# Attention outputs on quarters of TensorE: two PSUM banks for two units, and their weights fetched in one transfer

## The chip, the cores and the metric

The kernel runs on one core of a Trainium2 chip. The metric is the device time of one execution in microseconds (us); the kernel before takes 574.62 us, the median of three runs (573.59 to 574.97). TensorE (PE) multiplies matrices, VectorE (DVE), ScalarE (ACT) and GpSimd (POOL) work on elements, and SyncE (SP) issues nearly all DMA transfers from one queue, in order. TensorE writes only into PSUM, which has eight banks of 2 KB per partition.

## The reference, cut to what matters

```python
# q, k, v: (4, 8, 768, 64); 8 memory keys/values per head; chunks of 32 queries
for c in range(nc):
    k_ctx = k[:, :, max(0, c*32 - 16):min(S, c*32 + 32 + 8)]      # v_ctx likewise
    k_full = np.concatenate([mem_k, k_ctx], axis=2)               # 64 keys or fewer; v_full likewise
    scores = scale * np.matmul(q_c, k_full.transpose(0, 1, 3, 2))
    a = np.exp(scores - np.max(scores, axis=-1, keepdims=True))
    a = a / (np.sum(a, axis=-1, keepdims=True) + 1e-09)
    out[:, :, c_start:c_end] = np.matmul(a, v_full)               # the product that is changed
x = out.transpose(0, 2, 1, 3).reshape(B * S, H * D)
h = x @ w_in                                                      # (3072, 512) @ (512, 2048)
g = np.maximum(h, 0.0) + alpha * np.minimum(h, 0.0)
y = g @ w_out
```

Each chunk of 32 queries sees 64 keys: 16 to its left, its own 32, 8 to its right and the 8 memory keys.

## The kernel before, in words

The 3072 tokens are worked in eight half-sequences of 384 (`BT`). A *unit* is one half-sequence of two heads, so there are 32 units of twelve chunks each: four tiles of 96 queries (`TQ`), three chunks to a tile. Units 0 to 7 (`windows`) are worked in the first 30 us on their own path. Units 8 to 31 are the *later units*, and the change concerns these alone. They go in twelve pairs (`attend`), and of each pair:

- `head_products` (L425) multiplies 32 queries with their 64 keys, 24 matmuls per unit, each on 64 rows and 32 columns of TensorE; `scores` and `weights` make the softmax on DVE, ACT and POOL.
- `turn` transposes the weights of the two units on DVE into the tile `et` and writes them to DRAM (`far_e`); `fetch_turned` reads them back as `pt` with the keys on partitions. Before, a tile of 96 queries has its 104 keys and some more on 128 partitions, so every chunk's 64 keys go to another place among them (`PIECES`, four transfers) and the rest of `pt` is zero (`zero`, one memset on POOL at the sixth step of the first block, `CLEAR`).
- `value_products` (L528) multiplies the values `v_t` (loaded by `load_v` from `vw`) with `pt`: per unit eight matmuls (four tiles, two heads), each 128 keys by 64 dimensions with 96 columns of queries. Head 0 writes partitions 0 to 63, head 1 partitions 64 to 127. Each unit has one PSUM bank of its own (`bank`).
- `copy_raw` (L602) copies the unit's 384 columns from PSUM to SBUF on ACT, where POOL and ACT make further forms of them.

Most of TensorE's time goes to the two large products in fp32r as sums of three matmuls (high and low parts): L840 and L870 for the first blocks, L1311, L1418, L1274 and L1372 for the others, which use sums and differences of weight blocks.

The order on every engine is written by a planner (`Plan`): a step has an engine, a cost, what it reads and writes and how far it is from the end (`behind`), and the planner plays the steps through, on each engine taking the ready step with the largest `behind`. `SHIFT` adds a number to single steps, by name and count, and so moves them within the order. A planned cost is only what the planner reckons with.

Of the kernel before, what the change touches and what calls it, by code (L numbers as in the profile page):

```python
# [62 lines left out]
PIECES = [(0, 0, KW, 0), (1, 0, KW, CH), (2, 0, WIN, 2 * CH + NM), (2, WIN, KW, CH)]  # L63
# [54 lines left out]
CLEAR = 5  # L118

# [12 lines left out]
NV = NT * 2 * D  # L132

# [6 lines left out]
SHIFT = {("load_head", 1): 1.6, ("load_head", 7): 1.5, ("load", 0): 4.1, ("load", 4): -11.2, ("load", 15): 3,  # L140
         ("top", 0): 3, ("inverse", 0): -4.5, ("scale", 0): -1.5, ("scale", 1): -18, ("low", 0): -106.4,
         ("score_products", 1): 15, ("scale", 3): -12, ("keep", 2): -3, ("low", 1): 5.9, ("top", 2): 3,
         ("exps", 2): 3, ("total", 2): 1.5, ("inverse", 2): -0.8, ("scale", 5): 0.8, ("turn", 3): 6, ("keep", 6): 3,
         ("values", 3): 0.8, ("high", 3): 1.5, ("less", 4): -61.5, ("turn", 4): 6, ("values", 4): -12,
         ("keep", 11): -1.5, ("low", 5): -0.8, ("keep", 13): 6, ("high", 6): -11.2, ("total", 7): 0.8,
         ("keep", 15): -3, ("low", 7): 12.8, ("load", 22): 1.5, ("load", 28): 12, ("ends", 0): 9.8, ("up", 2): -1.5,
         ("low", 10): -12, ("gather", 2): 2.3, ("up", 15): 6, ("rebias", 4): -1.5, ("gather", 5): -21.7,
         ("ends", 4): 6, ("gather", 7): -3, ("high", 19): -3, ("low", 20): -12, ("low", 25): -1.5, ("up", 23): 12,
         ("high", 27): -12, ("up", 24): -56.9, ("put", 10): -1.5, ("put", 11): -12, ("up", 25): 6, ("high", 30): 3,
         ("low", 31): 12.1, ("low", 33): -12.8, ("high", 34): 3, ("low", 34): -2.3, ("low", 36): -15,  # L150
         ("put", 18): 1.5, ("low", 38): -3, ("products", 0): 101.5, ("top", 9): -0.8, ("up", 33): -3,
         ("inverse", 8): -1.5, ("get", 3): 0.8, ("exps", 28): 3, ("below", 23): -1.5, ("go", 2): -12,
         ("exps", 32): -1.5, ("put", 28): -6, ("below", 24): -6, ("bend", 25): 1.5, ("put", 43): -27.8,
         ("put", 44): -6, ("up", 41): 3, ("send", 4): -1.5, ("exps", 56): -12.8, ("inverse", 17): -12, ("go", 17): 3,
         ("high", 78): -3, ("low", 79): 0.8, ("copy", 18): 9.7, ("go", 95): 1.5, ("guard", 13): -6, ("get", 22): -3,
         ("go", 115): 12, ("go", 142): -1.5, ("go", 143): -8.9, ("low", 100): 6, ("products", 7): 12,
         ("go", 161): -6, ("go", 165): 3, ("low", 103): -3, ("go", 166): -3, ("bend", 63): 12, ("copy", 24): -6,
         ("exps", 110): -3, ("full", 14): 12, ("low", 109): 12, ("exps", 116): -12.1, ("exps", 120): -6,
         ("exps", 122): 0.8, ("exps", 126): -6, ("load_qk", 20): 3, ("low", 118): -3, ("go", 223): 6, ("go", 241): 3,
         ("low", 135): 6, ("top", 28): -0.8, ("exps", 128): -1.5, ("exps", 135): -0.8, ("low", 141): -13.5,  # L160
         ("go", 278): -6, ("low", 142): -12, ("low", 143): 1.5, ("go", 297): -12, ("go", 299): -12,
         ("go", 307): -18.8, ("put_down", 15): 26.3, ("go", 327): -10.5, ("exps", 146): 1.5, ("exps", 147): -11.2,
# [87 lines left out]
def body(ctx: ExitStack, tc: tile.TileContext, vw, qkw, whole, heads, w_in, w_out, alpha, out):  # L250
# [24 lines left out]
    busy = turned.tile([P, DM], BF16, name="busy", tag="et")  # L275
# [211 lines left out]
    def turn(u):  # L487
        v = u // 2
        et = {}

        def go(i):
            if i == 0:
                et[0] = turned.tile([P, 2, NJ, 2, 2, CH], F32, name="et", tag="et")
            nc.vector.transpose(out=et[0][:, :, :, :, i].rearrange("p k j h q -> p (j h) k q"),
                                in_=state[u + i]["e"].rearrange("p n (k q) -> p n k q", k=2))

        def put_turned():
            move(out=far_e[v].rearrange("t (r k) j x -> (t r) (k j x)", k=2), in_=et[0].rearrange("p k j h u q -> p (k j h u q)"))
# [23 lines left out]
    def value_products(u):  # L522
        st = state[u]
        pool, tag, _ = bank(u)
        st["a"] = pool.tile([P, 512], F32, name="a_ps", tag=tag)
        for t in range(NT):
            for h2 in range(2):
                nc.tensor.matmul(  # L528
                    out=st["a"][h2 * D:(h2 + 1) * D, t * TQ:(t + 1) * TQ],
                    lhsT=vs[0][:, u % 2, t, h2, :],  # L530
                    rhs=pts[0][:, :, t, h2, u % NPT, :],
                    start=True, stop=True,
                )

    def attend(place, olds, news, at_=None):

        def outputs():
            for u in olds:
                value_products(u)
# [54 lines left out]
    def copy_raw(u, ak):  # L594
# [9 lines left out]
        step(ACT, 0.48, copy, reads=[ak], writes=[key])  # L604
# [590 lines left out]
    for j in range(4):  # L1195
        EXTRA.append(([("pt", x) for x in range(len(PIECES))], two("pt", lambda: turned.tile([P, 4, BT], F32, name="pg", tag="pt"), j)))
# [3 lines left out]
    for j in range(2):  # L1200
        EXTRA.append(([("v", 0), ("v", 1)], two("v", lambda: ld.tile([P, 2, BT], F32, name="vg", tag="v"), j)))
# [3 lines left out]
    for j in range(2):  # L1205
        EXTRA.append(([("et", 0), ("et", 1)], two("et", lambda: turned.tile([P, 2, BT], F32, name="etg", tag="et"), j)))
    EXTRA.append(([("rs", 0, 0), ("rs", 0, 1)], two("r", lambda: sums.tile([P, 1, BT], F32, name="rg", tag="r"), 0)))

    def big(s):
# [370 lines left out]
        def meet(v, banks):  # L1580
# [5 lines left out]
            for u in olds:  # L1586
                copy_raw(u, bank(u)[2])
# [111 lines left out]
    for blk, f in ORDER:  # L1699
# [23 lines left out]
        for u in olds:  # L1723
            split(u, bank(u)[2])
# [22 lines left out]
_ORDER = ["vw", "qkw", "whole", "heads", "w_in", "w_out", "alpha"]  # L1747


def _layout(q, k, v, mem_k, mem_v, moe_w_in, moe_w_out, moe_alpha):  # L1750
# [11 lines left out]
    vwin = vwin.reshape(B, NPAIR, 2, nh, NT, P, D).transpose(0, 3, 1, 5, 4, 2, 6)  # L1762
# [40 lines left out]
```

## Time and profile before

| | us |
|---|---|
| median of three runs | 574.62 |
| the profiled execution, its own time | 574.95 |
| its span, first to last instruction | 573.2 |
| PE busy | 562.8 (98%) |
| DVE, ACT, POOL busy | 428.2, 311.5, 195.3 |

The profile is of one execution. "Busy" counts the time in which an engine works on something; a busy PE is not PE at its peak, since matmuls overlap and their ends are modelled. An fp32 matmul of the program stands in the trace as two records, each with its weight load (PEld), so eight matmuls of a unit are 16 records; an fp32r matmul is one. The granted clock is that of the higher level (2.4 GHz) all the time.

### The profile page before, as it was taken

The numbers are of one execution on the slowest core, as the hardware profiler recorded it, in microseconds if no ns is written. First come the engines' busy times: TensorE is split into PE (matmuls) and PEld (weight loads), VectorE is DVE, ScalarE is ACT, GpSimd is POOL, SyncE is SP. The second block draws the span as 40 slices with busy tenths as digits, with TensorE's granted clock in tenths as the row PEclk, the third lists the DMA queues.
The fourth block names the chain that finished last, engine by engine and source line by source line (L and its number), as shares of the span: only waits on it lengthen the run. The fifth ranks groups of instructions, "written<-read, shape, count | busy, mean of one in ns | idle before, by whom it ended". The sixth has DMA issues, their size and how long they took to land.

```text
span 573.2 us, 12065 instructions
## 1 busy us (share of the span) xinstructions
PE 562.8 (98%) x4515; PEld 509.2 (89%) x4515; DVE 428.2 (75%) x786; ACT 311.5 (54%) x792; POOL 195.3 (34%) x219
## 2 busy tenths in 40 slices
PE   7999999999999999999999999999999999999997
PEld 4789989888988899988888989999888899999997
DVE  7888888886648987666656777786855867787765
ACT  3778788775655663354566553543554543335452
POOL 5641000024375833005146511232533844443300
PEclk9999999999999999999999999999999999999999
DMA  8999954658996699987999999997988599778721
GB/s 310 374 417 419 414 238 184 227 216 293 335 377 251 231 393 409 377 322 259 326 365 331 351 382 327 355 313 287 312 290 280 198 339 353 279 241 332 266 84 56
DMA packets 64706, 173.57 MB, mean 303 GB/s; under 512 B 5768, under 2 KB 32520, under 8 KB 57736
## 3 DMA queue, kind: packets, MB, share of 16 engines
q1 hardware_dynamic: 64504, 172.70, 82.8%
q8 instruction: 36, 0.59, 0.4%
q14 instruction: 22, 0.18, 0.1%
q10 hardware_dynamic: 144, 0.10, 0.1%
HBM read 128.74 MB, written 44.04 MB: 301 GB/s over the span
## 4 chain that ended last, share of the span: by engine, by line
PE 88%; DMA 7%; DVE 2%; POOL 1%; issue 1%; ACT 0%; SPq 0%; DVEq 0%; POOLq 0%; ACTq 0%
PE b_ps L1418 25%; PE b_ps L1274 20%; PE o_ps L870 12%; PE h_ps L840 12%; PE b_ps L1372 10%; PE a_ps L528 3%; PE b_ps L1311 3%; DMA far_sS<-form 2%; PE s_ps L425 2%; DMA early<-heads 2%; DMA wa<-far_a 2%; DMA w_t<-w_out 1%; DVE u L1439 1%; PE a_ps L688 0%; POOL ew L663 0%
## 5 line engine op out<-in xcount | busy, mean ns | idle before, releaser
L1418 PE MATMUL b_ps<-xf,wa 128*128 128x384 f32 x924 | 168.1, 336 | 0.9 <-DMA wa<-far_a 0.9
L1418 PEld LDWEIGHTS b_ps<-xf,wa 128*128 128x128 f32 x924 | 161.1, 188 | 4.3 <-DVE gs L1235 1.3
L1439 DVE TENSOR_TENSOR u<-b_ps,u 128x384 f32<-128x384 f32 x154 | 79.5, 552 | 42.9 <-PE b_ps L1418 28.1
L1232 ACT ACTIVATE g<-u 128x384 f32<-128x384 f32 x88 | 45.5, 525 | 74.2 <-DVE u L1439 72.3
L480 POOL TENSOR_TENSOR e<-e,den 128x384 f32<-128x384 f32 x24 | 22.0, 919 | 137.5 <-DVE den L474 103.3
L840 PE MATMUL h_ps<-xh,w 128*128 128x384 f32 x256 | 65.4, 336 | 0.0
L1274 PE MATMUL b_ps<-wo,xh 128*128 128x512 f32 x180 | 55.9, 392 | 0.0
L1274 PE MATMUL b_ps<-wo,gh 128*128 128x512 f32 x180 | 55.9, 392 | 0.0
L870 PE MATMUL o_ps<-w,xh 128*128 128x512 f32 x168 | 52.5, 394 | 0.0
L840 PEld LDWEIGHTS h_ps<-xh,w 128*128 128x128 f32 x256 | 46.4, 188 | 0.8
L459 ACT ACTIVATE e<-s_ps,mx 128x64 f32<-128x64 f32 x144 | 43.1, 323 | 5.3 <-DVE mx L451 5.3
L840 PE MATMUL h_ps<-xl,w 128*128 128x384 f32 x128 | 43.7, 341 | 0.0
L1073 POOL TENSOR_TENSOR plain<-plain 128x384 f32<-128x384 f32 x24 | 29.4, 1238 | 36.6 <-ACT plain L602 29.7
L1274 PEld LDWEIGHTS b_ps<-wo,xh 128*128 128x128 f32 x180 | 33.8, 188 | 6.6
L1274 PEld LDWEIGHTS b_ps<-wo,gh 128*128 128x128 f32 x180 | 33.8, 188 | 6.5
L870 PEld LDWEIGHTS o_ps<-w,xh 128*128 128x128 f32 x168 | 31.5, 188 | 6.2
L1274 PE MATMUL b_ps<-wo,xl 128*128 128x512 f32 x90 | 35.4, 393 | 0.7 <-DVE xl L1252 0.7
L1274 PE MATMUL b_ps<-wo,gl 128*128 128x512 f32 x90 | 35.6, 395 | 0.0
L870 PE MATMUL o_ps<-w,xl 128*128 128x512 f32 x84 | 33.1, 394 | 0.0
L459 ACT ACTIVATION_READ_ACCUMULATOR e<-s_ps,mx 128x1 f32 x144 | 31.0, 215 | 0.0
L1059 POOL TENSOR_TENSOR xf<-plain,xf 128x384 fp32r<-128x384 f32 x24 | 27.0, 1142 | 11.3 <-ACT xf L1055 11.2
L852 DVE SCALAR_TENSOR_TENSOR g<-g,rise,h_ps 128x384 f32<-128x384 f32 x32 | 19.3, 607 | 12.5 <-ACT g L849 12.5
(166 smaller groups left out, 1129.6 us busy)
## 6 DMA issues: line engine op xcount, KB each, us to landing
wo<-far_o SPq DMA_DIRECT2D x24, 1024.0 KB
wa<-far_a SPq DMA_DIRECT2D x22, 1024.0 KB
wa<-far_b SPq DMA_DIRECT2D x22, 768.0 KB
qk<-qkw SPq DMA_DIRECT2D x24, 464.0 KB
w_t<-w_in SPq DMA_DIRECT2D x16, 512.0 KB
w_t<-w_out SPq DMA_DIRECT2D x16, 512.0 KB
far_o<-w SPq DMA_DIRECT2D x16, 512.0 KB
far_sS<-form SPq DMA_DIRECT2D x32, 256.0 KB
```

The source lines that it names most:

```text
L459: nc.scalar.activation(out=st["e"][:, i], in_=st["s"][h2][:, n], func=AF.Exp, scale=SCALE, bias=d["mx"][:, u - us[0], n, h2:h2 + 1], accum ...
L480: nc.gpsimd.tensor_tensor(out=st["e"], in0=st["e"], in1=st["den"].broadcast_to([P, NJ * 2, KW]), op=ALU.mult)
L840: nc.tensor.matmul(out=h["ps"][:, :BT], lhsT=ws[f, 0][:, wk, k * P:(k + 1) * P], rhs=parts(blk, k)[1](xk), start=(k == 0 and n == 0), stop ...
L852: nc.vector.scalar_tensor_tensor(out=h["g"], in0=h["g"], scalar=rise[:, f:f + 1], in1=h["ps"][:, :BT], op0=ALU.mult, op1=ALU.add)
L870: nc.tensor.matmul(out=o_ps[tt], lhsT=h[gk][:, tt * P:(tt + 1) * P], rhs=ws[f, 1][:, wk], start=(f == first_f and i == 0), stop=(f == last ...
L1059: eng.tensor_tensor(out=xf[x][:, 1, p], in0=plain_at(ap), in1=xf[x][:, 0, p].bitcast(F32), op=ALU.subtract)
L1073: step(POOL, 1.04, lambda: nc.gpsimd.tensor_tensor(out=plain_at(to[0]), in0=plain_at(a[0]), in1=plain_at(b[0]), op=ALU.subtract), reads=[a ...
L1232: nc.scalar.activation(out=h[name], in_=src(), func=AF.Relu, scale=-1.0)
L1274: nc.tensor.matmul(out=o[which][tt], lhsT=h[gk][:, tt * P:(tt + 1) * P], rhs=w[:, wk].bitcast(F32R), start=(f == turns[which][0] and i == ...
L1372: nc.tensor.matmul(out=o[0][bank[1]], lhsT=w[:, wk, m * P:(m + 1) * P].bitcast(F32R), rhs=forms_g[gk][xk], start=opened and k == 0, stop=c ...
L1418: nc.tensor.matmul(out=h[bank[1]][:, :BT], lhsT=weight(wk, p).bitcast(F32R), rhs=xf[xi][:, xk, p], start=p == 0 and k == 0, stop=p == 1 an ...
L1439: nc.vector.tensor_tensor(out=h[t], in0=h[bank[1]][:, :BT], in1=h[t if of is None else of], op=ALU.add)
```

## The change

`PIECES`, `CLEAR` and `zero` go. The host lays out the values once more (`vc`), with the 64 keys of each chunk on 64 partitions: tiles 0 and 2 on partitions 0 to 63, tiles 1 and 3 on 64 to 127. `pt` comes back in one transfer for the two units. A unit's products are now 24 matmuls of 64 keys by 64 dimensions with 32 columns: the half of the partitions (which tile) and the head choose one of four quarters of TensorE. The two halves of the partitions write two different banks, and both units write both, side by side; so every unit is copied with two ACT instructions of 192 columns, one from each bank, and both wait for the products of both units. `et` is now the second half of the tile `pt`, and `busy` has a place of its own. The planner's cost for the products goes from 0.73 to 0.65 per unit, for the copy from 0.48 to 0.68. Spare rooms for later results (`EXTRA`) move from `et` to `v_t`. The whole table `SHIFT` is another.

```diff
-    ("scale", 1): -18, ("low", 0): -106.4, ...
+    ("scale", 1): 0.8, ("low", 0): -104.9, ...
...
-            vs[0] = ld.tile([P, 2, NT, 2, D], F32, name="v_t", tag="v")
-            move(out=vs[0].rearrange("p u t h d -> p u (t h d)"), in_=vw[blk, pr:pr + 2].rearrange("u p x -> p u x"))
+            vs[0] = ld.tile([P, 2, NT // 2, NJ, 2, D], F32, name="v_t", tag="v")
+            move(out=vs[0].rearrange("p u a j h d -> p (u a j h d)"), in_=vc[(u - NWIN) // 2])
...
-                et[0] = turned.tile([P, 2, NJ, 2, 2, CH], F32, name="et", tag="et")
+                if not pts:
+                    pts.append(turned.tile([P, 2, NVC], F32, name="pt", tag="pt"))
+                et[0] = pts[0][:, 1].rearrange("p (k j h u q) -> p k j h u q", k=2, j=NJ, h=2, u=2)
...
-        def get(j, lo, hi, to):
-            move(out=pts[0][to:to + hi - lo, j].rearrange("p t h u q -> p t (h u q)"),
-                 in_=far_e[v][:, lo:hi, j].rearrange("t r x -> r t x"))
-
-        for n, x in enumerate(PIECES):
-            step(SP, 0, partial(get, *x), reads=[("ed", v)], writes=[("pt", n)], rest=rest(ends(u)))
+        def get():
+            move(out=pts[0][:, 0].rearrange("p (a x) -> p a x", a=NT // 2), in_=far_e[v].rearrange("(a t) r j x -> (t r) a (j x)", t=2))
+
+        step(SP, 0, get, reads=[("ed", v)], writes=["pt"], rest=rest(ends(u)))
...
-        st["a"] = pool.tile([P, 512], F32, name="a_ps", tag=tag)
-        for t in range(NT):
-            for h2 in range(2):
-                nc.tensor.matmul(
-                    out=st["a"][h2 * D:(h2 + 1) * D, t * TQ:(t + 1) * TQ],
-                    lhsT=vs[0][:, u % 2, t, h2, :],
-                    rhs=pts[0][:, :, t, h2, u % NPT, :],
-                    start=True, stop=True,
-                )
+        pairs = [bank(u) for u in us]
+        if us[0] % 2 == 0:
+            both = state[us[0]]["a"] = [pool.tile([P, 512], F32, name="a_ps", tag=tag) for pool, tag, _ in pairs]
+            state[us[0] + 1]["a"] = both
+        weights_at = pts[0][:, 0].rearrange("p (a j h u q) -> p a j h u q", a=NT // 2, j=NJ, h=2, u=NPT)
+        for u in us:
+            for a in range(NT // 2):
+                for j in range(NJ):
+                    at_ = ((u % 2) * NT // 2 + a) * TQ + j * CH
+                    for half in range(2):
+                        keys = slice(half * KW, (half + 1) * KW)
+                        for h2 in range(2):
+                            nc.tensor.matmul(
+                                out=state[u]["a"][half][h2 * D:(h2 + 1) * D, at_:at_ + CH],
+                                lhsT=vs[0][keys, u % 2, a, j, h2, :],
+                                rhs=weights_at[keys, a, j, h2, u % NPT, :],
+                                start=True, stop=True,
+                            )
...
-            nc.scalar.copy(out=plain_at(to), in_=st["a"][:, :BT])
+            x = plain_at(to).rearrange("p (a t q) -> p t a q", t=2, q=TQ)
+            at_ = (u % 2) * BT // 2
+            for t in range(2):
+                nc.scalar.copy(out=x[:, t], in_=st["a"][t][:, at_:at_ + BT // 2].rearrange("p (a q) -> p a q", q=TQ))
...
-            step(POOL, 1.6, zero, reads=[("w", 1, f, 1)], writes=[("ew", i) for i in range(NPT)] + [
-                ("pt", i) for i in range(len(PIECES))])
```

The first place is on TensorE in the middle of the program, the fifth of the twelve pairs (L528 before, L535 now, out of `v_t` and `pt`), with the waits of each row: PE's queue before.

```order
L1274 MATMUL b_ps<-wo,xl 128x512
L1274 MATMUL b_ps<-wo,xh 128x512 x2
L528 MATMUL a_ps<-pt,v_t 64x96 [waits DMAHW5_49,DMAHW6_49,DMAHW4_49,DMAHW7_49,DMAHW1_49,DVE_49]
L528 MATMUL a_ps<-pt,v_t 64x96 x7
L528 MATMUL a_ps<-pt,v_t 64x96 [waits DVE_49]
L528 MATMUL a_ps<-pt,v_t 64x96 x7
L1418 MATMUL b_ps<-xf,wa 128x384 [waits DMAHW0_49,DVE_49]
L1418 MATMUL b_ps<-xf,wa 128x384 x5
L1418 MATMUL b_ps<-xf,wa 128x384 [waits Activation_49]
L1418 MATMUL b_ps<-xf,wa 128x384 x5
```

And the same place in the changed kernel, where L1276 and L1420 are the lines that were L1274 and L1418.

```order
L535 MATMUL a_ps<-pt,v_t 64x32 [waits DMAHW6_49,DMAHW0_49,DVE_49]
L535 MATMUL a_ps<-pt,v_t 64x32
L535 MATMUL a_ps<-pt,v_t 64x32 [waits DVE_49]
L535 MATMUL a_ps<-pt,v_t 64x32 x45
L1420 MATMUL b_ps<-xf,wa 128x384 [waits DMAHW7_49,DVE_49]
L1420 MATMUL b_ps<-xf,wa 128x384 x5
L1276 MATMUL b_ps<-wo,gl 128x512 [waits DVE_49]
L1276 MATMUL b_ps<-wo,gh 128x512 [waits Activation_49]
L1276 MATMUL b_ps<-wo,gh 128x512
L1276 MATMUL b_ps<-wo,gl 128x512
L1276 MATMUL b_ps<-wo,gh 128x512 x2
L1420 MATMUL b_ps<-xf,wa 128x384 [waits PE_49,Activation_49]
```

Sixteen matmuls become 48, and six matmuls of L1276 now stand between the first product after the pair and the second, which needs a bank that ACT has to empty; before, the second product came right behind the first.

The second place is SP's queue around the first pair's return of the weights (`far_e` out and `pt` back), first before.

```order
L322 DMA qk_189<-qkw 128x928
L322 DMA qk_190<-qkw 128x928
L322 DMA pt<-far_e_196 8x4x128
L322 DMA pt<-far_e_196 64x4x128 x2
L322 DMA pt<-far_e_196 56x4x128
L322 DMA far_b_249<-form 128x1024
```

And now.

```order
L322 DMA qk_189<-qkw 128x928
L322 DMA qk_190<-qkw 128x928
L322 DMA pt<-far_e_196 128x2x384
L322 DMA far_b_249<-form 128x1024
L322 DMA far_a_241<-form 128x1024
```

Three issues fewer stand ahead of the transfers behind them, here and at each of the eleven other pairs.

## Rows read from the trace of the kernel before

**Rows 1.** The page: busy time of TensorE; its slices and its clock.
```profile
PE 562.8 (98%) x4515; PEld 509.2 (89%) x4515; DVE 428.2 (75%) x786; ACT 311.5 (54%) x792; POOL 195.3 (34%) x219
PE   7999999999999999999999999999999999999997
PEclk9999999999999999999999999999999999999999
```

**Rows 2.** Busy time by stretch: length, engines (instructions), clock, DMA share, GB/s.
```profile
0.00:30.00 30.00, 24.53 (x351) 17.60 (x352) 24.00 (x61) 15.94 (x35) 18.14 (x42) 1.00 0.94 345
30.00:140.00 110.00, 110.00 (x849) 98.88 (x848) 94.89 (x146) 83.78 (x177) 14.48 (x14) 1.00 0.77 296
140.00:280.00 140.00, 139.94 (x1312) 126.84 (x1311) 98.55 (x195) 73.86 (x238) 56.48 (x59) 1.00 0.90 332
280.00:360.00 80.00, 79.08 (x744) 69.21 (x744) 55.91 (x114) 43.59 (x140) 29.03 (x30) 1.00 1.00 348
360.00:440.00 80.00, 79.31 (x545) 69.97 (x541) 56.70 (x101) 36.34 (x89) 25.89 (x28) 1.00 0.90 316
440.00:574.00 134.00, 129.96 (x732) 126.67 (x728) 98.12 (x170) 57.94 (x117) 51.33 (x46) 1.00 0.65 232
```

**Rows 3.** Waits of TensorE, whole span: us in total, times, longest.
```profile
PE h_ps L385 <- DVE busy L283: 2.0, 1, 2.0
PE s_ps L401 <- DVE e L642: 1.1, 2, 1.0
PE b_ps L1418 <- DMA wa<-far_a: 0.9, 1, 0.9
PE b_ps L1274 <- DVE xl L1252: 0.7, 1, 0.7
```

**Rows 4.** Chain of waits in order of time, 200 to 300 us: start, us, what.
```profile
204.58 8.32 PE b_ps L1418 x48
...
285.68 1.47 PE a_ps L528 x32
287.15 8.40 PE b_ps L1274 x36
```

**Rows 5.** Timeline of TensorE, 102 to 106 us: a block of L425.
```profile
103.34 1.22 PE L425 MATMUL s_ps<-qk 64*32 64x64 f32 x96
104.49 0.44 PE L840 MATMUL h_ps<-xl,w 128*128 128x384 f32 x1
```

**Rows 6.** Line 425, 103 to 105 us: durations min/median/max in ns, starts.
```profile
L425 PEld LDWEIGHTS s_ps<-qk x96: 102/105/111, 103.3 to 104.3; 64*32 64x32 f32 x96
L425 PE MATMUL s_ps<-qk x96: 214/222/248, 103.3 to 104.3; 64*32 64x64 f32 x96
```

**Rows 7.** Line 528, 285 to 288 us.
```profile
L528 PEld LDWEIGHTS a_ps<-pt,v_t x32: 133/137/138, 285.6 to 286.8; 128*64 128x64 f32 x32
L528 PE MATMUL a_ps<-pt,v_t x32: 245/246/297, 285.6 to 286.9; 128*64 128x96 f32 x32
```

**Rows 8.** Line 401, weight loads of one product, 20.2 to 21.3 us.
```profile
L401 PEld LDWEIGHTS s_ps<-early x24: 106/110/111, 20.2 to 20.7; 128*32 128x32 f32 x24
```

**Rows 9.** Groups of ACT and POOL by shape: busy us, mean ns, idle before.
```profile
L602 ACT COPY plain<-a_ps 128x384 f32<-128x384 f32 x24 | 11.0, 478 | 12.2 <-PE a_ps L528 12.2
L1484 ACT COPY o_t<-b_ps 128x512 f32<-128x512 f32 x12 | 7.0, 586 | 3.7 <-PE b_ps L1274 3.0 <-DMA out<-o_t 0.7
L1073 POOL TENSOR_TENSOR plain<-plain 128x384 f32<-128x384 f32 x24 | 29.4, 1238 | 36.6 <-ACT plain L602 29.7 <-DVE mx L451 6.0 <-DVE xf L1059 0.6
```

**Rows 10.** Timeline of POOL, 40 to 48 us.
```profile
42.03 1.39 POOL L778 TENSOR_TENSOR w<-a,w 128x512 fp32r<-128x512 f32 x1 [5.01 <-ACT w L773]
43.36 1.39 POOL L713 MEMSET pt<- 128x1536 f32 x1
```

**Rows 11.** DMA issues: queue, count, KB each.
```profile
wa<-far_a SPq DMA_DIRECT2D x22, 1024.0 KB
v_t<-vw SPq DMA_DIRECT2D x12, 512.0 KB
pt<-far_e SPq DMA_DIRECT2D x24, 128.0 KB
pt<-far_e SPq DMA_DIRECT2D x12, 112.0 KB
pt<-far_e SPq DMA_DIRECT2D x12, 16.0 KB
```

**Rows 12.** Timeline of SP's queue, 125 to 160 us.
```profile
133.66 2.38 SPq L322 DMA_DIRECT2D pt<-far_e  x4
```

More of the change, by code (lines that the diff above doesn't have):

```diff
@@ L132 @@
 NV = NT * 2 * D
+NVC = NT // 2 * NJ * 2 * D
 NAPART = 2
 GATHER_ACT, HIGH_ACT = range(2, 14), 64
[L140 to L162, printed above, removed]
[9 rows of a table removed]
@@ new lines @@
+SHIFT = {("load_head", 9): -3, ("load_head", 11): -3, ("load_head", 12): -3, ("load", 0): 4.2, ("load", 6): -6,
+         ("load", 10): -6, ("load", 14): -0.8, ("top", 0): -0.8, ("less", 0): 1.4, ("total", 0): 6,
+         ("scale", 1): 0.8, ("low", 0): -104.9, ("score_products", 1): 6, ("exps", 1): 0.8, ("low", 1): 2.7,
+         ("less", 2): -1.5, ("scale", 5): 5.2, ("turn", 2): 12, ("high", 2): 3, ("low", 2): 1.5,
+         ("score_products", 3): 12, ("top", 3): 0.8, ("total", 3): -6, ("scale", 7): -3, ("keep", 6): -12,
+         ("values", 3): 6, ("less", 4): -37.5, ("scale", 11): 0.8, ("high", 5): 24, ("low", 5): 7.5, ("top", 6): 0.8,
+         ("inverse", 6): 6, ("scale", 12): -3, ("low", 7): 1.5, ("load", 18): 12, ("ends", 0): 1.5, ("up", 7): -3,
+         ("low", 12): -3, ("rebias", 3): 6.8, ("up", 10): 0.8, ("up", 14): 6, ("bend", 5): -12, ("gather", 7): -1.5,
+         ("join", 6): 6, ("join", 7): 3, ("low", 25): -3, ("low", 26): -0.8, ("up", 24): -56.9, ("low", 31): 16.6,
+         ("low", 32): 6, ("low", 33): -38.6, ("bend", 17): -4.5, ("high", 37): -12, ("put", 17): 3,
+         ("rebias", 13): 0.8, ("products", 0): 101.5, ("exps", 14): 1.5, ("gather", 25): 1.5, ("go", 1): 0.8,
+         ("put_turned", 0): -13.5, ("exps", 28): 0.7, ("high", 48): -6, ("low", 48): -0.8, ("exps", 32): -0.8,
+         ("full", 2): 6, ("merge", 4): 1.5, ("bend", 25): 6, ("outputs", 0): 2.2, ("full", 8): 1.5,
+         ("copy", 8): -1.5, ("scale", 23): -13.5, ("down", 31): -2.2, ("exps", 56): -10.6, ("exps", 72): 12,
+         ("exps", 73): -17.2, ("exps", 74): -5.2, ("high", 77): 0.8, ("go", 31): -3, ("scale", 26): -3,
[3 rows of a table added]
+         ("go", 181): -3, ("exps", 105): -6, ("high", 110): -6, ("full", 16): -3, ("go", 212): -9, ("high", 116): 3,
+         ("exps", 116): -12, ("exps", 125): -16.4, ("exps", 126): -1.5, ("exps", 127): 3, ("low", 118): -6,
+         ("go", 224): -6, ("high", 129): 6, ("below", 64): 3, ("exps", 132): -6, ("exps", 134): -23.3,
+         ("exps", 135): -1.5, ("go", 264): 10.5, ("low", 140): -3, ("go", 272): 13.5, ("below", 70): 3,
+         ("full", 18): -0.8, ("high", 142): -6, ("low", 142): 43.4, ("high", 143): 6, ("put_down", 10): -12,
+         ("bend", 74): -12, ("go", 304): 3, ("go", 306): -6, ("go", 307): -18.8, ("full", 20): 1.5,
+         ("go", 327): -9.7, ("go", 331): 0.8, ("put_down", 18): -0.8, ("load", 42): -0.8, ("exps", 145): -0.8,
+         ("exps", 146): -19.5, ("exps", 147): -12, ("exps", 149): -12, ("go", 336): -3, ("go", 338): 18.8,
[3 rows of a table added]
+         ("high", 185): 0.8, ("<lambda>", 16): 0.8, ("low", 188): -0.8, ("go", 496): -12, ("go", 510): -0.8,
+         ("high", 205): -1.5, ("less", 23): 1.5, ("low", 206): -0.8, ("high", 208): 0.8, ("less", 35): 12,
[3 rows of a table added]
@@ L500, in turn @@
         for i in range(2):
-            step(DVE, 0.6, partial(go, i), reads=e_keys(u + i), writes=[("et", 1)] if i else [("et", 0), ("et", 1)], rest=rest(ends(u)))
+            step(DVE, 0.6, partial(go, i), reads=e_keys(u + i), writes=[("et", 1)] if i else [("et", 0), ("et", 1), ("ew", 0), ("ew", 1)], rest=rest(ends(u)))
         step(SP, 0, put_turned, reads=[("et", 0), ("et", 1)], writes=[("ed", v)], rest=rest(ends(u)))
@@ L547, in attend @@
         if olds:
-            step(PE, 0.73 * len(olds), outputs,
-                 reads=[x for u in olds for x in [("v", u % 2)] + [("pt", i) for i in range(len(PIECES))]],
+            step(PE, 0.65 * len(olds), outputs,
+                 reads=[("v", u % 2) for u in olds] + ["pt"],
                  writes=[bank(u)[2] for u in olds] + ["met"], rest=rest(due_at))
@@ L1195, in body @@
     for j in range(4):
-        EXTRA.append(([("pt", x) for x in range(len(PIECES))], two("pt", lambda: turned.tile([P, 4, BT], F32, name="pg", tag="pt"), j)))
+        EXTRA.append((["pt", ("et", 0), ("et", 1)], two("pt", lambda: turned.tile([P, 4, BT], F32, name="pg", tag="pt"), j)))
     for i in range(4):
@@ L1199, in body @@
                       two(("e", i), lambda i=i: at.tile([P, 1, BT], F32, name="eg", tag=f"e{i}"), 0)))
-    for j in range(2):
-        EXTRA.append(([("v", 0), ("v", 1)], two("v", lambda: ld.tile([P, 2, BT], F32, name="vg", tag="v"), j)))
+    for j in range(4):
+        EXTRA.append(([("v", 0), ("v", 1)], two("v", lambda: ld.tile([P, 4, BT], F32, name="vg", tag="v"), j)))
     for i in range(NKB):
@@ L1586, in meet @@
             for u in olds:
-                copy_raw(u, bank(u)[2])
+                copy_raw(u, [bank(x)[2] for x in olds])
                 if u % 2 and u + 1 < NU:
@@ L1723, in body @@
         for u in olds:
-            split(u, bank(u)[2])
+            split(u, [bank(x)[2] for x in olds])
             if u % 2 and u + 1 < NU:
```

30 lines of the change are left out of this document (12 added, 18 removed), and 18 rows, old and new, of the table SHIFT.

## Prediction, made before the changed kernel ran

> **What bounds the kernel now.** I read the page first: TensorE is busy for 562.8 of 573.2 us, in all slices but the first and last at nine tenths or more, at the full clock throughout [rows 1]. By stretches, from 30 to 280 us PE is busy for 249.94 of 250 us, while DVE, ACT and POOL all have room [rows 2]. Then the waits: behind the first 30 us PE waits only 0.9 us for a DMA (`wa` from `far_a`) and 0.7 us for DVE; the other waits stand in the first 30 us, before the changed work begins [rows 3]. So the kernel is bound by what TensorE has to execute. An edit pays by the TensorE time it removes, and costs only where it makes PE wait.
>
> **TensorE: the value products.** A block (the products of two units) runs from 285.68 us to 287.15, the next group's start: 1.47 us, and there are twelve blocks [rows 4]. It is 32 records, whose starts lie 1.3 us / 31 = 42 ns apart [rows 7]. Each record streams 96 columns through one of two halves of the array, so a half takes a record every 84 ns: 0.87 ns per column.
>
> A changed block has 48 matmuls per two units times two records = 96 records, each with 32 columns, over four quarters. Streaming alone would be 96 x 32 x 0.87 / 4 = 0.67 us. But nothing in the trace says that streaming will set the pace. The nearest row is L425: also 64 rows deep, also 96 records in a block, 64 columns each over eight places. By streaming it would need 96 x 64 x 0.87 / 8 = 0.67 us as well; it takes 1.15 us, from 103.34 to 104.49 [rows 5], with starts 1.0 us / 95 = 10.5 ns apart [rows 6]. So something that goes by the record and not by the column sets that pace, and I take 1.15 us as the lower end.
>
> The weights set the upper end. L425 loads 32 columns per record, the changed block 64. At equal depth (128 rows) a load of 32 columns takes 110 ns [rows 8] and one of 64 takes 137 ns [rows 7]: 27 ns for 32 columns, so 64 columns occupy their quarter for about 54 ns. If loads on one quarter follow one another, the 96/4 = 24 of a quarter need 24 x 54 = 1.30 us, and with the 0.15 us that L425's block has beyond its starts, 1.45 us. That would be no gain. I take the middle, 1.30 us: the depth, the alternation of places and the number of records are L425's, which speaks for its pace, and the wider loads speak against it. The term is 12 x (1.47 - 1.30) = -2.0 us, with ends 12 x 0.32 = -3.8 and 12 x 0.02 = -0.2.
>
> The Trainium skill has a rule against this change: TensorEngine Tiling (Array Packing), section Instruction Overhead, says that each matmul carries about 60 cycles, so that very few columns cost as much as some 60, and that no tiling should be taken from a dimension that is already small. Taken as a spacing between any two matmuls that is 25 ns at the full clock, and the block would be an estimated 96 x 25 = 2.4 us. The trace does not agree with that spacing: L425's records start 10.5 ns apart [rows 6]. What it may still hold for is the time of a record on its own quarter; that is a rival below.
>
> **ACT: the copies.** 24 copies of 384 columns at 478 ns become 48 of 192. A copy of 512 columns takes 586 ns, so 128 columns are 108 ns and 192 columns are 478 - 162 = 316 ns [rows 9]. ACT gets 24 x (632 - 478) = 3.7 us more, with 54% of the span in use. What could reach PE is the later release of the two banks: both are free only after four copies, 1.26 us behind the block, where it was 0.96 for two. In the order of the changed kernel PE has one product (six matmuls of L1420, 48 of which took 8.32 us: 1.04) and six of L1276 (36 took 8.40: 1.40) ahead of the first product that needs such a bank [rows 4]; at the other pairs it is two of these groups or more. 2.4 us cover 1.26, so the wait costs 0; were the cover gone, 0.3 us per block, 3.6 in all. POOL's forms wait for the copies, 29.7 us in four waits [rows 9], but POOL is busy for a third of the span and these waits are of products that are late anyway: 0.
>
> **POOL: the memset.** 1.39 us at 43.36, with POOL idle for 5.01 us just before it [rows 10] and PE not waiting at all from 30 to 140 us [rows 2]: 0.
>
> **SP and the DMA.** `pt` comes in one transfer of 384 KB in place of 16 + 128 + 128 + 112 KB [rows 11]; the four issues held SP's queue for 2.38 us at the first pair [rows 12]. `v_t` becomes 768 KB in place of 512. At the 348 GB/s of the stretch with the fullest queues [rows 2], 256 KB more are 0.75 us per pair, 9 us of DMA time over the whole run; three issues fewer per pair win back about 1.8 us of the queue's issuing each. PE waits for a DMA only 0.9 us in all [rows 3], so the most that a smoother queue can give is 0.9. I take 0, between -0.9 and +2.
>
> **The order.** The table `SHIFT` moves single steps on every engine. Behind 30 us there are 1.6 us of PE waits to win [rows 3]; ahead of it the 3.1 us in the two lines named belong to the first units' path, whose PE order is unchanged up to the first large products; I take 0, between -1.5 and +2.
>
> **The sum** is 574.95 us for the profiled execution, 2.0 less: 572.95. That execution lies 0.33 us above the median, so against 574.62 the forecast is 572.6 us. I count as the same what lies within 0.3% (1.7 us), about what a measurement of this kernel can tell from no change.
>
> **Rivals.**
> 1. *L425's pace is reached.* The wider loads are hidden behind the other quarters' streams, as L528's loads of the same width are hidden in its 84 ns per half [rows 7]. Then 12 x 0.32 = 3.8 us go: 570.8. Against it: a quarter has only 27 ns of streaming to hide 54 ns of loading.
> 2. *The loads set the pace.* A block takes 1.45 us, and the time is 574.4, the same. For it: loads of one quarter must follow one another. Against it: no row shows a pace set by loads.
> 3. *Slower: a narrow record costs its place as much as a wide one.* In L425 each of eight places takes a record every 8 x 10.5 = 84 ns, though 64 columns stream in 56: as if load (27) and stream (56) came one after the other. If a quarter needs the same 84 ns for a record of 32 columns (load 54 and stream 28 are 82 too), a block takes 24 x 84 = 2.0 us and 0.15: 2.17 us, 0.70 more than before, +8.4 us: 583.0. That is what the skill's rule would mean here. Against it: in L528 load and stream of a half would add to 54 + 84 = 138 ns, and a record is done in 84, so there they overlap [rows 7]. It decides from a block of 1.62 us on, where the loss passes 1.7 us.
> 4. *Slower: the DMA wait grows.* In 280 to 360 us the DMA share is 1.00 [rows 2], and the one DMA wait of PE lies there. If five pairs' larger `v_t` pushed the weights `wa` back by 0.75 us each, +3.8 against -2.0: 576.4. It decides once PE's waits for `far_a` pass 0.9 + 3.7 us. Against it: the transfer of `pt` loses its small pieces.
>
> **How the numbers follow.** The forecast's case (blocks of 1.2 to 1.4 us, 571.3 to 573.8 us) 0.42, rival 1 0.18, rival 2 0.21, rival 3 0.10, rival 4 0.09. Faster by over 0.3% means below 572.9: about 0.29 of the forecast's 0.42 and all of rival 1, 0.47. Slower by over 0.3% is above 576.3: all of rival 3 and some two thirds of rival 4 and of bad orders, 0.17. The rest, 0.36, is the same. The range runs from 569.8 (rival 1 with 1 us of the order's waits won) to 577.2 (rival 4 with 0.8 us of the order's waits lost); rival 3 stays outside.
>
> **What would show it.** In the profile after, a block should begin a new group 1.2 to 1.4 us after its first record, with record starts 11 to 13 ns apart; 1.45 and more means that the loads set the pace, 2 us that load and stream follow one another on a quarter. PE's waits behind 30 us should stay under 2 us, none of them for ACT's copies of `plain`. The copies should take 0.30 to 0.34 us each. Wrong would be the reasoning, not only a size, if the blocks shrink and the span does not follow, for then PE waits somewhere that I put at nothing.

## The result, and the profile after

The changed kernel takes 578.43 us (median of four runs, 577.99 to 578.94), the kernel before 574.74 beside it. The ratio is 1.0069, with an interval of 1.0051 to 1.0086: slower by 0.7%. The forecast was 572.6, and the time lies above the range. The profiled execution took 577.99 us; its span is 576.2, 3.0 more than before.

The page of the changed kernel: span, busy time, TensorE's clock, and the queue that carries TensorE's instructions (q8): packets, MB, share of the DMA engines.

```profile
span 576.2 us, 13572 instructions
PE 562.4 (98%) x5283; PEld 511.0 (89%) x5283; DVE 430.5 (75%) x786; ACT 314.3 (55%) x816; POOL 189.8 (33%) x218
PEclk9999999999999999999999999999999999999999
q8 instruction: 42, 0.69, 0.5%
```

TensorE is busy for 0.4 us less than before [rows 1] and yet ends 3.0 us later, so there are new waits. In this execution the clock is the higher level throughout, as before (the three others show a mean of 0.997 and have no profile). TensorE's 768 added records, each with its load, are 1536 instructions, and q8 has six packets more than the 36 on the page before: 0.69 MB / 42 = 16 KB, so one packet for 1536 / 6 = 256 instructions.

TensorE's waits over the whole span: us in total, times, longest.

```profile
PE s_ps L401 <- DMA early<-vw: 2.7, 1, 2.7
PE a_ps L535 <- issue: 2.1, 2, 1.8
PE h_ps L385 <- DVE busy L283: 2.0, 1, 2.0
PE s_ps L401 <- DMA early<-heads: 1.7, 3, 0.8
PE s_ps L401 <- DVE mx L647: 0.9, 1, 0.9
PE b_ps L1420 <- issue: 0.8, 1, 0.8
```

Both waits that the kernel before had behind 30 us (0.9 for `wa`, 0.7 for DVE [rows 3]) are gone. In their place stand three for "issue", that is, for nothing that the profile shows: two of 2.1 us together and one of 0.8. TensorE's timeline shows where (start, us, what, idle before it in brackets). The first pair:

```profile
143.32 1.22 PE L425 MATMUL s_ps<-qk 64*32 64x64 f32 x96
144.47 1.00 PE L535 MATMUL a_ps<-pt,v_t 64*64 64x32 f32 x52
147.27 0.32 PE L535 MATMUL a_ps<-pt,v_t 64*64 64x32 f32 x8 [1.79 <-issue]
```

The ninth and the tenth:

```profile
329.23 1.59 PE L535 MATMUL a_ps<-pt,v_t 64*64 64x32 f32 x92
331.15 0.30 PE L535 MATMUL a_ps<-pt,v_t 64*64 64x32 f32 x4 [0.34 <-issue]
...
363.40 1.19 PE L425 MATMUL s_ps<-qk 64*32 64x64 f32 x96
364.52 3.92 PE L1420 MATMUL b_ps<-xf,wa 128*128 128x384 f32 x21
369.29 0.44 PE L1420 MATMUL b_ps<-xf,wa 128*128 128x384 f32 x1 [0.84 <-issue]
```

And a block that nothing disturbs, then the durations of the copies of all twelve pairs (min/median/max in ns):

```profile
176.32 1.60 PE L535 MATMUL a_ps<-pt,v_t 64*64 64x32 f32 x96
177.85 0.50 PE L874 MATMUL o_ps<-w,gl 128*128 128x512 f32 x1
```

```profile
L611 ACT COPY plain<-a_ps x48: 310/326/354, 148.1 to 441.7; 128x192 f32<-128x192 f32 x48
```

A block takes 177.85 - 176.32 = 1.53 us where it took 1.47 [rows 4], so each is 0.06 longer. The copies take 326 ns; the forecast was 300 to 340.

**What the waits have in common.** Counted from the start, the first wait ends 1360 matmuls and 1360 loads into the program, the one in the tenth pair 4023 and 4023 in (stretch, then busy us and count of each engine):

```profile
0.00:147.20 147.20, 138.15 (x1360) 120.55 (x1360) 122.86 (x217) 102.98 (x215) 35.36 (x60) 1.00 0.81 310
0.00:331.10 331.10, 321.69 (x3644) 284.39 (x3645) 252.73 (x465) 204.59 (x555) 110.00 (x138) 1.00 0.88 327
0.00:369.20 369.20, 358.99 (x4023) 319.33 (x4023) 281.12 (x525) 221.95 (x611) 116.06 (x147) 1.00 0.89 331
```

TensorE's queue has some records more that are neither; with these, counted in the trace, the numbers are 2753, 7361 and 8129. They lie 18 x 256 and 3 x 256 apart: each wait sits on a border between two blocks of 256 instructions, which I call pages. The page before the first wait was entered at 143.46 us and its last instruction began at 145.3. The only packet of q8 from 143 to 147.3 us starts at 144.84 and takes 947 ns:

```profile
q8 instruction: 1, 0.02, 11.8%
```

(That is 144.5 to 145 us.) So the reading, theory F, is this: only one page is fetched ahead, its fetch starts around the time when the page before it is entered or some us later, and where that page is over before the next is there, TensorE waits. A page that holds mostly short instructions I call dense. Scores and values side by side are 192 + 192 instructions in under 2.7 us, and the page before the first wait holds nothing else.

Density is not all of it. The pages before the ninth and tenth pair's waits lasted 5.7 and 5.0 us, and their packets started only 4.0 us after they were entered (328.86 against 324.89, 367.09 against 363.12). In the kernel before the value block is 64 instructions. Its shortest page, also in the tenth pair, lasts 4.9 us and is as dense as the changed kernel's there (218 and 211 of 256 instructions are scores and values), but its packet started 1.3 us after the entry, and nothing waits. So in the tenth pair it is the later fetch that makes the wait; why it is later was not tested.

The Trainium skill, Runtime: NRT & Kernel Launch, section Instruction fetch mechanics, says that instructions come in blocks of 256, the next while the current one runs, and that crossing a border is mostly hidden. The trace agrees on the 256 and differs on the hiding at three borders: 1.79, 0.34 and 0.84 us here.

### The profile page after: what moved, and what is told of

It reads as the page before. It is cut to its first block, busy times and chain, and to the rows that moved or that the text cites. A ratio compares the mean times of both kernels' runs of the same rounds, so it can differ in the third digit from the quotient of the medians.

```text
span 576.2 us, 13572 instructions
## 1 busy us (share of the span) xinstructions
PE 562.4 (98%) x5283; PEld 511.0 (89%) x5283; DVE 430.5 (75%) x786; ACT 314.3 (55%) x816; POOL 189.8 (33%) x218
## 4 chain that ended last, share of the span: by engine, by line
PE 96%; DMA 2%; POOL 1%; issue 1%; SPq 0%; DVE 0%; DVEq 0%; POOLq 0%
PE b_ps L1420 28%; PE b_ps L1276 23%; PE h_ps L844 12%; PE o_ps L874 12%; PE b_ps L1374 10%; PE a_ps L535 3%; PE b_ps L1313 3%; PE s_ps L425 2%; DMA early<-heads 1%; PE a_ps L697 1%; PE o_ps L684 1%; DMA early<-vw 1%; POOL early L280 1%; PE s_ps L401 0%; POOL ew L302 0%
## 5 line engine op out<-in xcount | busy, mean ns | idle before, releaser
L1420 PE MATMUL b_ps<-xf,wa 128*128 128x384 f32 x924 | 168.5, 336 | 0.9 <-issue 0.8
L1420 PEld LDWEIGHTS b_ps<-xf,wa 128*128 128x128 f32 x924 | 161.1, 188 | 4.3 <-issue 1.2
L1276 PE MATMUL b_ps<-wo,gh 128*128 128x512 f32 x180 | 55.9, 392 | 0.0
L1276 PE MATMUL b_ps<-wo,xh 128*128 128x512 f32 x180 | 55.9, 392 | 0.0
L1276 PEld LDWEIGHTS b_ps<-wo,xh 128*128 128x128 f32 x180 | 33.8, 188 | 6.7
L1276 PEld LDWEIGHTS b_ps<-wo,gh 128*128 128x128 f32 x180 | 33.8, 188 | 6.5
L1077 POOL TENSOR_TENSOR plain<-plain 128x384 f32<-128x384 f32 x24 | 27.7, 1173 | 35.6 <-ACT plain L611 35.6
L1276 PE MATMUL b_ps<-wo,gl 128*128 128x512 f32 x90 | 35.7, 397 | 0.0
L1276 PE MATMUL b_ps<-wo,xl 128*128 128x512 f32 x90 | 35.1, 390 | 0.0
L989 POOL TENSOR_TENSOR form<-form 128x256 f32<-128x256 f32 x17 | 13.3, 782 | 49.1 <-DVE form L986 26.1
```

Of the source, the lines that this page charges most:

```text
L1077: step(POOL, 1.04, lambda: nc.gpsimd.tensor_tensor(out=plain_at(to[0]), in0=plain_at(a[0]), in1=plain_at(b[0]), op=ALU.subtract), reads=[a ...
L1276: nc.tensor.matmul(out=o[which][tt], lhsT=h[gk][:, tt * P:(tt + 1) * P], rhs=w[:, wk].bitcast(F32R), start=(f == turns[which][0] and i == ...
L1420: nc.tensor.matmul(out=h[bank[1]][:, :BT], lhsT=weight(wk, p).bitcast(F32R), rhs=xf[xi][:, xk, p], start=p == 0 and k == 0, stop=p == 1 an ...
```

## The experiments

Theory F is that account. Its rivals are that the waits belong to the new form of the products or to their place (P), and that the loss is in the new front order. Theory L says that the blocks' 1.53 us are set by weight loads; R that they go by the record, S that they go by streamed columns.

**Dense blocks apart.** Where two dense blocks would follow one another on TensorE, the next other step of the plan is put between them.

```diff
-            fn()
+            if engine == PE:
+                dense = getattr(fn, "func", fn).__name__ in ("outputs", "products")
+                if dense and self.dense and not self.held:
+                    self.held.append(fn)
+                else:
+                    fn()
+                    for late in self.held:
+                        late()
...
```

> The changed kernel, with one PE step put between a block of score products (L425) and a block of value products wherever the two stand next to each other: 12 matmuls ahead of the first pair's values, 6 between the tenth pair's values and the scores behind them. Theory F (PE's queue runs out of fetched instructions where two dense blocks adjoin): the wait of 1.79 us within the first pair's block and that of 0.84 us behind the tenth pair go, the one of 0.34 us in the ninth pair's block stays; 578.4 - 2.6 = 575.8 us, 575.2 to 576.6. Rival D (the block waits for data: pt, v_t or a bank is late): the first wait shrinks by what the block now comes later, 2.1 us, so it goes too, but the one behind the tenth pair, where no operand changes, stays; 576.6. Rival O (the time went to the table's other moves): no change, 578.4.

Measured: 577.12 us, ratio 1.0041 (1.0027 to 1.0054), span 575.3. Its waits of TensorE:

```profile
PE h_ps L856 <- DVE g L868: 1.3, 1, 1.3
PE h_ps L856 <- ACT plain L623: 1.1, 1, 1.1
...
PE b_ps L1432 <- issue: 0.5, 1, 0.5
```

The first pair's fetch wait is gone, but the values had filled a gap in which TensorE would wait for DVE, and their bank now comes free later: 2.4 us of other waits. The ninth pair's block is still 0.39 us longer than 1.53, as F expected; the wait at the tenth pair should have gone and is still 0.5 us, with 8129 instructions ahead of it as before. This alone can't tell F from P, since it moves the work.

**The count moved by 40.** 20 small matmuls (40 instructions) are added while TensorE waits for its first data; the order stays.

```diff
...
+            stir(t, num)
+            for _ in range(20 if u == 0 else 0):
+                nc.tensor.matmul(out=t[:, :8], lhsT=busy[:, :P], rhs=busy[:, :8], start=True, stop=True)
```

> The changed kernel with 20 tiny bf16 matmuls (40 instructions on PE) more at the program's start, in the same order otherwise. Theory F: instructions come in pages of 256, so each page's border stands 40 instructions earlier: the first pair's block stops after record 32 instead of 52, the ninth after 72 instead of 92, the tenth pair's wait comes about 20 records earlier than the 21st matmul of L1420; the waits stay of a like size and the time within 1 us of 578.4. Rival D: a wait for data stays where it is, after record 52, 92 and 21.

Measured: 580.9 us, ratio 1.0108 (1.0078 to 1.0137), span 578.8. TensorE's timeline at the first, the ninth and the tenth pair:

```profile
144.11 1.60 PE L538 MATMUL a_ps<-pt,v_t 64*64 64x32 f32 x96
...
326.77 1.25 PE L538 MATMUL a_ps<-pt,v_t 64*64 64x32 f32 x72
328.21 0.55 PE L538 MATMUL a_ps<-pt,v_t 64*64 64x32 f32 x24 [0.19 <-issue]
...
359.79 0.99 PE L538 MATMUL a_ps<-pt,v_t 64*64 64x32 f32 x55
360.71 1.19 PE L428 MATMUL s_ps<-qk 64*32 64x64 f32 x96
361.83 0.61 PE L1423 MATMUL b_ps<-xf,wa 128*128 128x384 f32 x2
366.53 1.33 PE L1423 MATMUL b_ps<-xf,wa 128*128 128x384 f32 x3 [4.09 <-issue]
```

The waits stay with the count: in the ninth pair the wait stands behind record 72, as F expected, and the one at the tenth is at 8129 instructions again, now 19 matmuls earlier in the work. That speaks for F and against P. The sizes came out otherwise than expected: the first pair waits for nothing, though its page lasted 1.6 us, because the fetch started at 142.07, 0.9 us before that page was entered; at the tenth pair the page lasted 1.98 us and the fetch started 4.1 us after its entry.

The time is 2.5 us above the changed kernel's, and the longer wait is not all of it. While TensorE stood still, the granted clock fell to the lower level (1.2 GHz), at 364.1 us, and it came back at 370.9. The stretch, with the busy time of each engine and then the clock:

```profile
364.20:370.90 6.70, 4.37 (x14) 4.37 (x15) 1.70 (x5) 1.01 (x3) 2.79 (x4) 0.50 0.76 308
```

So the 4.4 us of work behind the wait went at half the clock, an estimated 2.2 us more.

**Kinds of blocks.** In the changed kernel single pairs get another form: the third 32 of the 64 dimensions (`[:32]` of `v_t`), the fourth 16 of the 32 queries, the fifth all matmuls of one quarter in a row, the sixth and seventh another order of the quarters, the eighth two of the quarters only, the ninth both halvings, the eleventh 64 streamed columns. Attention outputs are thus left incomplete or false in these pairs; it is one execution (583.5 us), read for the lengths of its blocks alone.

```diff
+        if kind in ("d32", "d32q16"):
+            dims = D // 2
+        if kind in ("q16", "d32q16"):
+            num = CH // 2
...
+                row = 0 if kind == "two" else half
+                keys = slice(row * KW, (row + 1) * KW)
...
+                    out=state[u]["a"][half][h2 * D:h2 * D + dims, at_:at_ + num],
+                    lhsT=vs[0][keys, u % 2, a, j, h2, :dims],
+                    rhs=weights_at[keys, a, j, h2, u % NPT, :num],
```

> The changed kernel with another form of the value products in several pairs, so that the blocks' lengths can be read side by side; the results of these pairs are not the reference's. Pairs 2, 10 and 12 as they are (1.53 us). Pair 3: 32 of 64 dimensions (weight loads of 32 columns). Pair 4: 16 of 32 queries (half the streaming). Pair 5: twelve records in a row on one quarter. Pairs 6 and 7: the four quarters in two other orders. Pair 8: all on the same 64 rows, so two quarters for 96 records. Pair 9: 32 dimensions and 16 queries. Pair 11: 64 columns streamed. Theory L (a quarter's loads of 64 columns follow one another, some 54 to 58 ns each, and set the pace): pairs 3 and 9 take 1.15 us, pairs 4, 6, 7 stay at 1.53, pair 8 takes 2.9, pair 5 at least 3, pair 11 1.5 to 1.7. Rival R (a cost of 14.5 ns per record whatever it does): all 1.53. Rival S (load and stream of a quarter add up): pair 4 faster by a fifth, pair 11 2.3 us.

Measured, from the start of a block to the next group's, on TensorE's timeline; third, fourth, fifth, eighth and eleventh pairs (the second, as in the changed kernel, takes 1.53):

```profile
176.04 1.02 PE L561 MATMUL a_ps<-pt,v_t 64*32 64x32 f32 x96
176.99 0.50 PE L900 MATMUL o_ps<-w,gl 128*128 128x512 f32 x1
...
190.82 1.59 PE L561 MATMUL a_ps<-pt,v_t 64*64 64x16 f32 x96
192.34 0.50 PE L1302 MATMUL b_ps<-w,xl 128*128 128x512 f32 x1
...
225.72 4.33 PE L561 MATMUL a_ps<-pt,v_t 64*64 64x32 f32 x96
229.99 0.81 PE L1446 MATMUL b_ps<-xf,wa 128*128 128x384 f32 x3
...
306.12 2.99 PE L561 MATMUL a_ps<-pt,v_t 64*64 64x32 f32 x96
309.04 0.71 PE L1302 MATMUL b_ps<-wo,gl 128*128 128x512 f32 x1
...
428.93 1.63 PE L554 MATMUL a_ps<-pt,v_t 64*64 64x64 f32 x96
430.49 0.50 PE L1302 MATMUL b_ps<-wo,gl 128*128 128x512 f32 x1
```

Half the dimensions, that is, half the columns of weights: 0.95 us for the same 96 records, so R falls. Half the streamed columns: 1.52, twice as many: 1.56, so S falls. So the pace goes with the weight loads. The sixth and seventh take 1.54. One quarter at a time takes 4.27, two quarters 2.92. L had given 1.15 for the third pair, so its picture of one quarter's loads in a row does not fit (last section). The ninth block has a fetch wait of 0.26 us inside and says nothing more.

**The front's old order.** The first run of these (dense blocks apart), with the entries of the kernel before for the front in `SHIFT`; the rest of the table stays:

```diff
-SHIFT = {("load_head", 9): -3, ... ("scale", 1): 0.8, ("low", 0): -104.9, ...
+SHIFT = {('up', 10): 0.8, ... ('scale', 1): -18, ('low', 0): -106.4, ...
```

> As e1_apart, and with the numbers of the table for the first units and the first decoded weights (SHIFT entries of the first 30 us) taken from the kernel before. Theory F plus the front (PE reaches the first pair's block 0.46 us later than before, by the order of the first loads): 0.4 us less than e1_apart, 575.4 us. If the front was paid back anyway: the same as e1_apart.

Measured: 578.15 us, ratio 1.0062 (1.0037 to 1.0087), span 576.9, no better than the first run's 1.0041. A fetch wait of 1.3 us stands at 8129 again, where the first run had 0.5, so the two times can't price 0.4 us of the front. The profiles say more. The scores of the first pair, which stand at the same place in the work, start at 142.84 us in the kernel before, 142.75 here and 142.15 in the kernel before made dense (below), all with the old front; and at 143.32 in the changed kernel, 142.03 in the first run and 142.67 in the run of kinds, with the new one. The two overlap: the 0.46 us is within the spread from one execution to another, and a loss by the front's order is not shown.

**Pages moved, meant to leave none dense.** 52 small matmuls at the start and 65 behind the first pair, in five groups of 13. The order stays.

```diff
+    def few(t, num):
+        for i in range(num):
+            c = i % 4 * 32
+            nc.tensor.matmul(out=t[c:c + 32, :8], lhsT=busy[:64, c:c + 32], rhs=busy[:64, :8], start=True, stop=True)
...
+            stir(t, num)
+            few(t, 52)
...
+    more = []
...
+        if us[0] // 2 == NWIN // 2:
+            more.extend([13] * 5)
...
                 h["ps"] = ps_h.tile([P, 512], F32, name="h_ps", tag=hk)
+                if more:
+                    few(h["ps"], more.pop())
```

> The changed kernel with its order of work kept, and only the count of TensorE's instructions moved: 52 small bf16 matmuls (32 columns of weights, 8 streamed) while TensorE still waits for its first data at the start, and 13 before each of five groups of the first product between the first and second pairs. Nothing else changes, the dense blocks stand side by side as before. Theory F (TensorE waits for its instructions when 256 of them, one page, are executed in under some 2 to 5 us): with 104 more instructions ahead of the first pair a page border falls in the middle of its dense area, and with 130 more behind it one falls in the middle of the tenth pair's; each page then holds ordinary products as well and lasts over 5 us. The issue waits (1.8 us in the first pair, 0.34 in the ninth, 0.84 in the tenth) go, the first block takes 1.5 us, and the span is 576.2 less 3.0 and plus 65 small matmuls of 11 to 35 ns (0.7 to 2.3 us): 573.9 to 575.5. Rival P (the waits belong to the place: to quarter blocks behind score products and the change of tile shape there): they stay where they are in the work, and the span is 576.9 to 578.5.

Measured: 577.32 us, ratio 1.0047 (1.0032 to 1.0062), span 575.6, where F gave 573.9 to 575.5 without any wait. The waits of the ninth and tenth pairs are gone and the first block is whole. One wait is left, and it is 256 instructions on, in the middle of the second group of my small matmuls:

```profile
144.65 1.60 PE L546 MATMUL a_ps<-pt,v_t 64*64 64x32 f32 x96
...
148.66 0.21 PE L390 MATMUL h_ps<-busy 64*32 64x8 bf16 x7
149.98 0.19 PE L390 MATMUL h_ps<-busy 64*32 64x8 bf16 x4 [1.12 <-issue]
```

The page from 144.64 held the values and 40 instructions of small matmuls and lasted 4.06 us; its successor's packet started 2.3 us after its entry and took 1.97 us. P falls: the wait has left the products and stands at a bf16 matmul.

**The kernel before, made dense.** 32 small fp32 matmuls are added to it ahead of the first pair's values, into a bank that these overwrite.

```diff
         st["a"] = pool.tile([P, 512], F32, name="a_ps", tag=tag)
+        for i in range(32 if u == NWIN else 0):
+            c = i % 4 * 32
+            nc.tensor.matmul(out=st["a"][c:c + 32, :CH], lhsT=vs[0][:64, 0, 0, 0, :32], rhs=pts[0][:64, 0, 0, 0, 0, :CH],
+                             start=True, stop=True)
```

> The kernel before, with 32 small fp32 matmuls (64 records of 32 columns of weights and 32 streamed) put between the scores and the values of the first pair, into a bank that the values then overwrite. Theory F: the page that began at 142.98 us in the kernel before and lasted 5.73 us is now filled with dense records alone and lasts some 2 us; TensorE then waits 1 to 2.5 us for its instructions, at or just behind the first pair's values, where the kernel before waits for nothing. Span 573.2 plus 64 x 11 to 17 ns (0.7 to 1.1) plus the wait: 574.9 to 576.8. Rival P (the wait comes from the values' form, 64 keys on quarters, which this kernel doesn't have): no wait there, 573.9 to 574.3.

Measured: 578.34 us, ratio 1.0054 (1.0031 to 1.0077), span 576.5. TensorE's timeline, where L532 are the old products:

```profile
142.15 1.22 PE L425 MATMUL s_ps<-qk 64*32 64x64 f32 x96
143.18 0.66 PE L528 MATMUL a_ps<-pt,v_t 64*32 64x32 f32 x51
145.69 0.32 PE L528 MATMUL a_ps<-pt,v_t 64*32 64x32 f32 x13 [1.85 <-issue]
145.94 1.54 PE L532 MATMUL a_ps<-pt,v_t 128*64 128x96 f32 x32
```

The kernel before gets the same wait, 1.85 us, once its page is dense, at instruction 2753. That is within what F gave (1 to 2.5) and shows that such a wait needs none of the change. Only part of the span's 3.3 us is this wait: TensorE's waits for `wa` and for DVE behind 30 us are 1.5 and 1.4 us here, and 0.9 and 0.7 without the small matmuls. Nor does a dense page always wait, as the first pair showed where the count was moved by 40.

**The same, with the small matmuls in better places.** 13 ahead of the values of each of the second to sixth pairs, in place of the five groups.

```diff
             state[us[0] + 1]["a"] = both
+            few(both[0], 13 if 1 <= us[0] // 2 - NWIN // 2 <= 5 else 0)
```

> As the run before, but the second lot of 65 small matmuls stands elsewhere: 13 just before the values of each of the second to sixth pairs, away from the first pair's page. The 52 at the start stay. Theory F: the page that holds the first pair's values now holds 64 ordinary instructions beside 192 dense ones, 32 matmuls of 0.17 us, and lasts some 7 us; the one in the tenth pair's dense area likewise. No issue wait of TensorE is left behind 30 us; span 576.2 less 3.0 plus 65 x 19 ns (0.25 us for 13 in the run before), 1.2: 574.4, and with the blocks' 0.7 us over the kernel before the ratio comes to about 1.002. Rival Q (a wait of the sort comes somewhere on every path, because the fetch is late wherever the queues are full): waits of 1 to 2 us appear at another page border though its page lasts over 5 us, and the span is 575.5 to 577.

Measured: 575.49 us, the kernel before 575.28 beside it, ratio 1.0002 (0.9986 to 1.0019); span 573.9, where F gave 574.4. All waits of TensorE that the view lists:

```profile
PE s_ps L408 <- DMA early<-heads: 2.9, 2, 2.6
PE h_ps L385 <- DVE busy L283: 2.0, 1, 2.0
PE s_ps L408 <- DVE mx L655: 0.6, 1, 0.6
PE s_ps L408 <- DVE den L670: 0.5, 1, 0.5
```

All four stand in the first 30 us; behind them the view lists no wait of TensorE, and Q falls with P. The tenth pair, before with 0.84 us:

```profile
360.50 1.60 PE L543 MATMUL a_ps<-pt,v_t 64*64 64x32 f32 x96
362.03 1.19 PE L432 MATMUL s_ps<-qk 64*32 64x64 f32 x96
363.15 3.06 PE L1428 MATMUL b_ps<-xf,wa 128*128 128x384 f32 x16
```

117 matmuls of no use make the changed kernel 0.7% faster, because the borders of pages fall elsewhere. It equals the kernel before; no version here beats it.

## Why the prediction was wrong

- **The value products** (middle 1.30 us a block). This step failed. I chose the middle because L425 has as many records, and as many records do not mean the same pace: at 32 columns of weights the block takes 0.95 us, at 64 it takes 1.53. Rival 2 was right that the loads set the pace, and its 1.45 was near; but its working, 24 loads of one quarter at 54 ns each and 0.15, is not what the runs show. A round of four quarters takes 1.53 / 24 = 64 ns, and one quarter alone needs 44 ns a record. 12 x (1.53 - 1.30) = 2.8 us of the miss. With 1.53 the forecast would have been 0.7 us slower than before, which counts as the same.
- **What was not in the sum: instruction fetch.** This step failed too: I put TensorE's waits behind 30 us at no more than before (under 2 us). I counted records per block to find a pace, and never asked whether the instructions themselves arrive. 1.79 + 0.34 + 0.84 = 3.0 us of waits. This turned "the same" into "slower", as the last run shows, where they are gone and the ratio is 1.0002. Either miss alone would have left the time within the range.
- **The order, SP and the DMA** (0 each). Behind 30 us the 1.6 us of old waits went, more than my 0; whether the shorter queue or the new order took away the 0.9 us for `wa` was not told apart. In the front 0.46 us came (the first block starts at 144.47, and before, with the same work behind it, at 144.01), which is within the spread of that place. My rival 4 fell: no wait for `far_a` grew.
- **ACT's copies** (316 ns, hidden). Measured 326, and no wait of TensorE for them. POOL's forms waited 35.6 us in place of 29.7, at no cost to TensorE. **The memset** went; TensorE had no wait for it, and no run prices it by itself.
- **Rival 3** fell: a block takes 1.53 us, not 2.17, and half the streamed columns change nothing.

The pieces of the two profiled executions: fetch +3.0, blocks 12 x 0.06 = +0.7, front +0.5, old waits -1.6, together +2.6 of the span's +3.0. Some 0.4 us are not assigned.

## What to carry to other kernels

When a change splits matmuls into many short ones, count instructions as well as time: find where 256 of TensorE's instructions in a row would pass in less than some 6 us, and expect that TensorE may wait there for the next page until the trace shows otherwise (here it waited behind pages of 1.4 to 5.7 us, and behind others of 1.6 to 5.7 us it did not, by when the fetch started). Waits marked "issue" whose instruction counts differ by multiples of 256 are most likely such waits, and moving the count by some small instructions where the engine is idle tests it, and can mend it. For small tiles, take the pace from a row that loads as many columns of weights, not one with as many records.

## What the runs showed of the hardware

- **The fetch's start varies.** Over the nine traces the packet started from 4.8 us before the page ahead of it was entered to 5.8 us after, 1.0 us after in the median, and took 0.96 us in the median (counted from q8's packets against TensorE's records). Where the DMA engines were busy for over 95% of the 2 us behind the entry, the median start was 2.2 us after it; where for less than half, 0.4. The spread within each is large, and what sets it stays open. It was not tried whether fewer transfers at that moment shorten it.
- **The wait ends well behind the packet.** In every case a wait of TensorE for its instructions ended 1.1 to 1.8 us after the packet had landed: 147.27 against 144.84 + 0.95 in the first pair, 145.69 against 143.28 + 0.89 in the kernel before made dense. From the packet's start until TensorE goes on, it is 2.2 to 3.1 us.
- **The clock can fall behind a long wait.** Besides the 4.09 us above, the last run shows the lower level (0.50) from 15.1 to 18.4 us, behind a wait of 2.6 us that ended at 14.1; the changed kernel has one of 2.7 us in the front and kept 1.00. What decides between the two was not tested.
- **Loads on the same 64 rows seem to follow one another, across quarters.** Four quarters take 1.53 / 24 = 64 ns a round, two quarters on the same rows 2.92 / 48 = 61, one alone 4.27 / 96 = 44. So it is not one quarter's loads that fill the 64 ns, as theory L had it, but more likely two loads of some 31 ns on the same rows, with the two halves of the rows side by side. The 0.95 / 24 = 40 ns of two 32-column loads and L425's 84 ns for four [rows 6] fit 20 to 21 ns each. The 44 ns of one quarter alone is more than one load of 31 and stays unexplained. That is a reading of four sizes; it was not tested by a run of its own.
